# Routed attention with an ELU layer: the second mask of the first half of q moves from GpSimd to ScalarE

## The chip, the core and the metric

The kernel runs on one core of a Trainium2 chip. A core has five engines that run their own queues in order: TensorE (PE in the profile; PEld is its load of weights), VectorE (DVE), ScalarE (ACT), GpSimd (POOL) and SyncE (SP), which here only issues DMAs. The metric is device time in microseconds, the median of several runs. The profile is of one further execution.

## What is computed

Attention in which a query sees only the keys of its own cluster, followed by two matrix products with an ELU between them:

```python
q_assign = np.argmax(np.einsum('bhsd,hcd->bhsc', q_n, c_n), axis=-1)
k_assign = np.argmax(np.einsum('bhsd,hcd->bhsc', k_n, c_n), axis=-1)
mask = q_assign[:, :, :, None] == k_assign[:, :, None, :]
scores = scale * np.matmul(q, k.transpose(0, 1, 3, 2))
scores = np.where(mask, scores, -1000000000.0)
scores = scores - np.max(scores, axis=-1, keepdims=True)
attn = np.exp(scores)
attn = attn / (np.sum(attn, axis=-1, keepdims=True) + 1e-09)
return np.matmul(attn, v).astype(np.float32)
...
h = x @ w_in
g = np.where(h > 0.0, h, alpha * (np.exp(np.minimum(h, 0.0)) - 1.0))
return (g @ w_out).astype(np.float32)
```

There are 4 batches, 8 heads, 768 positions, a head size of 64 and 16 clusters per head. The layer has 3072 tokens, 512 channels and 2048 hidden ones. All is float32.

## The kernel before, in words

The attention runs over 32 blocks: 4 batches, two halves of q (384 rows each), four pairs of heads. For a block and each of 6 tiles of 128 keys, TensorE makes two plain score products (L510, one per head of the pair) and adds two masked products (L523) into the same bank; ScalarE takes the exponential (L532); in the next block TensorE multiplies the results with v (L548). VectorE adds the exponentials up (L535, L540, L541). Three pairs of banks go round in a ring (`pair_tiles`).

The mask is a product too. `assign` (L446) makes a one-hot code of the clusters of each row: VectorE turns the similarities (L453), takes the maximum over 16 clusters (L455), compares each value with it (L456, which also counts the hits) and turns the 0/1 codes back (L466). L456 reads two tiles that lie in SBUF, `sim` and `top`; the others read one. Two copies on ScalarE (L469) then put each half of the partitions into the other half, as side 1 of `hot_k` or `hot_q`. `mask_q` (L474) makes from `hot_q` two tiles `q_mask[half][:, :, x]`, x = 0 and 1, each a multiplication and an addition with a scalar per partition (`big`, `minus`): 0 where the cluster is the row's own, a huge negative number elsewhere. Tile x serves the pairs of heads with pr % 2 = x, so x = 0 serves the first block and x = 1 the second. In `mask_q` the masks of the first half of q in the first batch (b = 0, half = 0) are made by GpSimd (L478), all later ones by ScalarE (L480).

The order of the work is written out by hand: each engine executes its instructions in the order in which the code names them. Work that is to go to ScalarE or GpSimd a little later is put into the list `later` and issued by `flush()`. The start is `slot_first` (L632). There q and k of the first batch are turned by TensorE (`turned`, L622: products with the identity, then a copy by ScalarE at L630), and in this order:

- q is turned, and its clusters are found (`clusters_q(0, 0, d_bank)()`); the copies of L469 and both masks are put into `later`.
- The first 512 columns of k are turned for all four pairs of heads, and the remaining 256 for the first pair.
- The similarities of k's first 512 columns are computed into `o_bank`.
- `flush()` at L647 issues the copies for q on ScalarE and both masks on GpSimd.
- The remaining 256 columns of k are turned for the other three pairs (L648, L649), with three copies on ScalarE.
- The plain products of the first key tile (L651) and the similarities of k's last 256 columns into `d_bank` (L652) follow on TensorE.
- `told[0]()` (L653) is `assign` for k's first 512 columns on VectorE; the flush after it issues the copies of L469 for them on ScalarE.
- `told[1]()` is the same for the last 256. After three loads of SyncE's queue have been named, the loop over the six key tiles begins (L660).

The first masked product (L523) of the first block needs `hot_k` from L466, the second one side 1 of it from the first copy of L469.

After the attention the layer is computed in blocks with sums of sub-matrices, on all engines; nothing of that is edited.

Of the kernel before, what the change touches and what calls it, by code (L numbers as in the profile page):

```python
# [61 lines left out]
def main_path(ctx, tc, c, q, k, v, centroids, moe_w_in, moe_w_out, out):  # L62
# [118 lines left out]
    def load_k(b, pr):  # L181
        in_blocks(raw_k[pr % 2], k[b, 2 * pr : 2 * pr + 2])

    def load_q(b, half):
        for pr in range(NPR):
            in_blocks(raw_q[pr], q[b, 2 * pr : 2 * pr + 2, ts(half, HS)])
# [102 lines left out]
    def ask():  # L289
        nonlocal asked  # L290
        while asked < len(pieces):
            to, src = pieces[asked]
            if not wide:
                if asked == into and split < into:
                    return
                nc.sync.dma_start(to, src)
                asked += 1
                continue
            places[:] = [x for x in places if asked < x[1]]
            if not places:  # L300
                return
            place, limit = places.pop(0)
            w = place.rearrange("p a n -> p (a n)") if place.shape[1] == 1 else place
            n = to.shape[1]
            if place.shape[1] == 1:
                w = w.rearrange("p (f n) -> p f n", f=n)
            elif n == 1:
                src = src.rearrange("p a (f n) -> p (a f) n", f=place.shape[1])
            w = w.bitcast(U32)
            nc.sync.dma_start(w, src.bitcast(U32))  # L310
            words[asked] = (w.rearrange("p f (n w) -> p f n w", w=2), place, limit)
            asked_in[asked] = now
            asked += 1
# [56 lines left out]
    half = FC // 2  # L370
# [33 lines left out]
    credit, later, powers = 0.0, [], []  # L404

    def flush(*of):
        for others in of or (later, powers):
            for other in others:
                other()
            others.clear()  # L410
# [25 lines left out]
    def similar(t, cols, ps):  # L436
        for pr in range(NPR):
            nc.tensor.matmul(  # L438
                ps[32 * pr : 32 * pr + 32, : cols.stop - cols.start],
                lhsT=cT[:, 32 * pr : 32 * pr + 32],  # L440
                rhs=t[pr][:, cols],
                start=True,
                stop=True,
            )

    def assign(hot, ps):  # L446


        nonlocal counted
        size = hot.shape[2]  # L450
        n = size // NC
        sim, oh, top = told_in[size]
        nc.vector.transpose(sim, ps[:, :size])  # L453
        s = sim.rearrange("p (n c) -> p n c", c=NC)
        nc.vector.tensor_reduce(top, s, axis=Axis.X, op=Alu.max)  # L455
        nc.vector.scalar_tensor_tensor(  # L456
            oh.rearrange("p (n c) -> p n c", c=NC),
            s,
            1.0,
            top.unsqueeze(2).to_broadcast([P, n, NC]),  # L460
            op0=Alu.mult,
            op1=Alu.is_equal,
            accum_out=count[:, counted : counted + 1],
        )
        counted += 1
        nc.vector.transpose(hot[:, 0], oh)  # L466
        for e in range(2):
            later.append(
                lambda e=e: nc.scalar.copy(  # L469
                    hot[64 * (1 - e) : 64 * (1 - e) + 64, 1], hot[64 * e : 64 * e + 64, 0]  # L470
                )
            )

    def mask_q(b, half):  # L474
        for x in range(2):
            to, by, more = q_mask[half][:, :, x], big[:, x : x + 1], minus[:, x : x + 1]
            if (b, half) == (0, 0):
                nc.gpsimd.tensor_scalar(to, hot_q, by, more, op0=Alu.mult, op1=Alu.add)  # L478
            else:
                nc.scalar.activation(to, hot_q, Act.Identity, scale=by, bias=more)  # L480

    def clusters_k(b, half, ps):
        cols = slice(half * HS, half * HS + HS)
        if b == 0:
            cols = slice(half * CUT, S if half else CUT)
        similar(kT[b % 2], cols, ps)
        return lambda: assign(hot_k[b % 2][:, :, cols], ps)

    def clusters_q(b, half, ps):
        similar(qT[half], slice(0, HS), ps)  # L490

        def told():
            assign(hot_q, ps)
            later.append(lambda: mask_q(b, half))

        return told

# [3 lines left out]
    def ring():  # L501
        nonlocal turn_of
        turn_of = (turn_of + 1) % 3
        return pair_tiles[turn_of]

    def plain(n, kt, s):
        b, half, pr = blocks[n]
        for e in range(2):
            rows = slice(64 * e, 64 * e + 64)
            nc.tensor.matmul(  # L510
                s[:, e, :HS],
                lhsT=kT[b % 2][pr][rows, ts(kt, P)],
                rhs=qT[half][pr][rows],
                start=True,
                stop=False,
            )

    def masked(n, kt, s):
        b, half, pr = blocks[n]
        for e in range(2):  # L520
            rows = slice(64 * e, 64 * e + 64)
            side = int(pr // 2 != e)
            nc.tensor.matmul(  # L523
                s[:, e, :HS],
                lhsT=hot_k[b % 2][rows, side, ts(kt, P)],
                rhs=q_mask[half][rows, side, pr % 2],
                start=False,
                stop=True,
            )

    def exponential(kt, s):
        nc.scalar.activation(probs[kt], s[:, :, :HS], Act.Exp, scale=SCALE)  # L532

    def sums_begin():
        nc.vector.tensor_tensor(  # L535
            add_to, probs_all[:, : 4 * HS], probs_all[:, 4 * HS : 8 * HS], op=Alu.add
        )
# [76 lines left out]
    def turned_by_pe(to, t, n):  # L614
        for h in range(2):
            nc.tensor.matmul(  # L616
                to[D * h : D * h + D], lhsT=t[:, h, n], rhs=ident, start=True, stop=True
            )
# [3 lines left out]
    def turned(to, t, n):  # L622

        nonlocal turns
        bank = pair_tiles[turns % 3][:, turns // 3 % 2]
        turns += 1
        size = to.shape[1]
        for i in range(size // P):
            turned_by_pe(bank[:, ts(i, P)], t, n + i)
        nc.scalar.copy(to, bank[:, :size])  # L630

    def slot_first():  # L632

        for _ in range(6):
            nc.tensor.matmul(
                o_bank, lhsT=blank, rhs=blank[:, 0:1].to_broadcast([P, 512]), start=True, stop=True
            )
        for pr in range(NPR):
            turned(qT[0][pr], first_q[pr], 0)
        nc.tensor.transpose(o_bank[:, :P], work[:, : 2 * D], ident)  # L640
        nc.vector.tensor_copy(cT, o_bank[:, :P])
        clusters_q(0, 0, d_bank)()
        for pr in range(NPR):
            turned(kT[0][pr][:, :CUT], first_k[pr], 0)
        turned(kT[0][0][:, CUT:], first_k[0], CUT // P)
        told = [clusters_k(0, 0, o_bank)]
        flush()  # L647
        for pr in range(1, NPR):  # L648
            turned(kT[0][pr][:, CUT:], first_k[pr], CUT // P)  # L649
        first = ring()  # L650
        plain(0, 0, first)  # L651
        told.append(clusters_k(0, 1, d_bank))  # L652
        told[0]()  # L653
        flush()
        told[1]()
        load_k(1, 0)
        ask()
        load_q(0, 1)
        load_k(1, 1)
        for kt in range(NT):  # L660
            s = ring() if kt else first
            if kt:
                plain(0, kt, s)
            masked(0, kt, s)
            exponential(kt, s)
            if kt == 2:
                flush()
            elif kt == 3:
                sums_begin()
# [432 lines left out]
    class OutUnit:  # L1102
        of, width = "out", P
# [53 lines left out]
    class InUnit:  # L1157
        of, width = "in", 512
# [343 lines left out]
    def verdict():  # L1502
# [4 lines left out]
        nc.vector.tensor_copy(c["go"], ps[:1, :1])  # L1507

    slot_first()
    for n in range(1, len(blocks)):  # L1510
        slot(n)
# [334 lines left out]
```

## Time and profile before

| | us |
|---|---|
| median of 3 runs (lowest, highest) | 890.75 (890.51, 891.31) |
| the profiled execution, its own time | 889.33 |
| its span, first to last instruction | 887.5 |
| busy in the span: PE, DVE, ACT, POOL | 876.4, 711.5, 446.0, 228.3 |

The profile is read through views. The page gives each engine's busy share in 40 slices of the span and the chain of work that ended last, followed back from the last instruction to what released it. The chain can also be listed in order of time. The timeline lists the instructions of an engine with their start, their length, how many were merged (x3), and in brackets the idle time before them and what ended it. The view of one line gives the durations of its instructions, each form with its shape. "L456" is line 456 of the kernel; names such as `p_out<-o_bank` are what is written and what is read. Some tiles share memory under another name: `hot_q`, `hot_k` and the raw k and q of the start lie in `w_out`, the masks in `kq_g`.

### The profile page before, as it was taken

To read this page: it belongs to the slowest core of one execution; us is meant where nothing else is said; L and a number is where in the kernel's file an instruction comes from. 1 tells how busy PE (TensorE), PEld (TensorE's weight loads), DVE (VectorE), ACT (ScalarE), POOL (GpSimd) and SP (SyncE) were. 2 spreads that over 40 slices of the span, in tenths; PEclk is the share of its full clock that TensorE was granted. 3 is DMA by queue.
4 is the path that set the end of the run, shared out by engine and by line. 5 is a ranking of instruction groups with operands and counts; after the bars stand their busy time and mean duration, and the time that the engine had idled before them with its cause. 6 is when DMAs were issued, how large, how long until landed. Compare 5 with 4: busy or idle time off the path is not lost.

```text
span 887.5 us, 17035 instructions
## 1 busy us (share of the span) xinstructions
PE 876.4 (99%) x6437; PEld 677.6 (76%) x6441; DVE 711.5 (80%) x1041; ACT 446.0 (50%) x852; POOL 228.3 (26%) x294
## 2 busy tenths in 40 slices
PE   8999999999999999999999999999999999999996
PEld 5444444444444458899989999999999999999996
DVE  4789998999998997898688957884788478856784
ACT  6678786787768654412233235423542364236421
POOL 1011121121113566841332013601351135103200
PEclk9999999999999999999999999999999999999999
DMA  7766685466337342165677875186518761866171
GB/s 239 169 129 184 148 180 135 122 125 146 80 120 213 126 143 64 49 163 135 217 247 247 274 217 167 57 278 212 176 52 273 216 186 48 267 214 192 42 244 68
DMA packets 157370, 145.68 MB, mean 164 GB/s; under 512 B 89824, under 2 KB 109280, under 8 KB 156256
## 3 DMA queue, kind: packets, MB, share of 16 engines
q1 hardware_dynamic: 151584, 132.45, 50.5%
q0 software_dynamic: 5408, 11.54, 5.7%
q8 instruction: 53, 0.87, 0.4%
q10 hardware_dynamic: 288, 0.52, 0.2%
q14 instruction: 37, 0.30, 0.1%
HBM read 114.59 MB, written 21.50 MB: 153 GB/s over the span
## 4 chain that ended last, share of the span: by engine, by line
PE 93%; POOL 3%; issue 2%; DVE 1%; DMA 0%; ACT 0%; SPq 0%; POOLq 0%; ACTq 0%
PE bank L1086 23%; PE banks L510 15%; PE o_bank L548 14%; PE bank L796 12%; PE bank L1176 9%; PE o_bank L1086 4%; PE banks L523 4%; PE o_bank L796 2%; PE d_bank L1086 2%; PE o_bank L1176 2%; PE d_bank L568 1%; PE d_bank L438 1%; POOL kq_g L810 1%; PE d_bank L1176 1%; PE banks L616 1%
## 5 line engine op out<-in xcount | busy, mean ns | idle before, releaser
L532 ACT ACTIVATE p_out<-banks 128x768 f32<-128x768 f32 x192 | 154.0, 811 | 25.4 <-PE banks L523 24.2
L548 PE MATMUL o_bank<-p_out,kq_g 128*64 128x384 f32 x768 | 130.9, 490 | 0.0
L548 PEld LDWEIGHTS o_bank<-p_out,kq_g 128*64 128x64 f32 x768 | 52.3, 137 | 74.7 <-issue 70.3
L810 POOL TENSOR_SCALAR kq_g<-kq_g 128x512 f32<-128x512 f32 x96 | 69.1, 728 | 109.7 <-ACT kq_g L809 108.3
L535 DVE TENSOR_TENSOR sums_w<-p_out 128x1536 f32<-128x1536 f32 x32 | 59.1, 1847 | 10.3 <-ACT p_out L532 10.3
L796 PE MATMUL bank<-xT,spare 128*128 128x256 f32 x256 | 59.2, 379 | 0.0
L809 ACT ACTIVATE kq_g<-bank 128x512 f32<-128x512 f32 x68 | 39.8, 602 | 38.5 <-PE bank L796 18.4
L540 DVE TENSOR_TENSOR sums_w<-sums_w,p_out 128x1536 f32<-128x1536 f32 x32 | 56.2, 1757 | 3.3 <-DVE sums_w L535 0.5
L609 POOL DMA_DIRECT2D sums_w<-xT x28 | 17.7, 649 | 153.2 <-DVE xT L585 92.0
L1086 PE MATMUL bank<-w_out,kq_g 128*128 128x128 f32 x448 | 56.0, 275 | 0.3 <-DVE kq_g L813 0.3
L1086 PEld LDWEIGHTS bank<-w_out,kq_g 128*128 128x128 f32 x448 | 53.4, 192 | 0.8 <-DVE kq_g L813 0.5
L796 PEld LDWEIGHTS bank<-xT,spare 128*128 128x128 f32 x256 | 48.3, 190 | 6.4
L796 PE MATMUL bank<-x_sum,w_in 128*128 128x256 f32 x224 | 52.9, 379 | 0.0
L813 DVE SCALAR_TENSOR_TENSOR kq_g<-kq_g,bank 128x512 f32<-128x512 f32 x68 | 45.0, 680 | 7.7 <-POOL kq_g L810 7.7
L1194 POOL TENSOR_TENSOR spare<-x_sum 128x128 f32<-128x128 f32 x16 | 7.3, 457 | 154.4 <-PE bank L1176 88.8
L796 PEld LDWEIGHTS bank<-x_sum,w_in 128*128 128x128 f32 x224 | 42.6, 190 | 5.8
L1390 DVE TENSOR_TENSOR kq_g<-kq_g 128x1024 f32<-128x1024 f32 x36 | 43.9, 1221 | 0.0
L562 ACT ACTIVATE xT<-o_bank 128x384 f32<-128x384 f32 x32 | 15.6, 489 | 53.0 <-PE o_bank L548 53.0
L604 POOL TENSOR_TENSOR xT<-xT,sums_w 128x384 f32<-128x384 f32 x32 | 41.1, 1304 | 1.6 <-DMA sums_w<-xT 1.6
L510 PE MATMUL banks<-x_sum,xT 64*128 64x384 f32 x192 | 39.8, 492 | 0.0
L510 PE MATMUL banks<-kq_g,xT 64*128 64x384 f32 x192 | 39.6, 491 | 0.0
L510 PE MATMUL banks<-kq_g 64*128 64x384 f32 x192 | 39.6, 491 | 0.0
(379 smaller groups left out, 2027.5 us busy)
## 6 DMA issues: line engine op xcount, KB each, us to landing
kq_g<-in_v_dram SPq DMA_DIRECT2D x32, 384.0 KB, 3.8
sums_w<-far_s_s SPq DMA_DIRECT2D x42, 256.0 KB, 3.7
spare<-w_far SPq DMA_DIRECT2D x32, 256.0 KB, 3.0
words_w<-far_s_s SPq DMA_DIRECT2D x26, 256.0 KB, 3.1
out_dram<-p_out SPq DMA_DIRECT2D x22, 256.0 KB, 3.2
w_out<-in_q_dram SPq DMA_DIRECT2D x112, 48.0 KB, 2.5
sums_w<-xT POOLq DMA_DIRECT2D x28, 192.0 KB, 3.3
sums_w<-far_s_q SPq DMA_DIRECT2D x21, 256.0 KB, 3.5
```

The lines of the kernel that those rows point to most:

```text
L510: nc.tensor.matmul(s[:, e, :HS], lhsT=kT[b % 2][pr][rows, ts(kt, P)], rhs=qT[half][pr][rows], start=True, stop=False,)
L532: nc.scalar.activation(probs[kt], s[:, :, :HS], Act.Exp, scale=SCALE)
L535: nc.vector.tensor_tensor(add_to, probs_all[:, : 4 * HS], probs_all[:, 4 * HS : 8 * HS], op=Alu.add)
L540: nc.vector.tensor_tensor(add_to, add_to, probs_all[:, 8 * HS :], op=Alu.add)
L548: nc.tensor.matmul(o_bank[64 * e : 64 * e + 64, :HS], lhsT=v_raw[n % 2][:, e, kt], rhs=probs[kt][:, e], start=(kt == 0), stop=(kt == NT - 1),)
L604: nc.gpsimd.tensor_tensor(x_of(n), x_of(n), r, op=Alu.mult)
L796: nc.tensor.matmul(bank[:, ts(f, QS)], lhsT=left[:, ch, ts(f, P)], rhs=right[:, ch], start=first and f == 0 and ch == 0, stop=ch == 1, ski ...
L810: nc.gpsimd.tensor_scalar(to, to, 1.0, 0.0, op0=Alu.min, op1=Alu.max)
L813: nc.vector.scalar_tensor_tensor(to, to, -1.0, as_part(bank, to), op0=Alu.add, op1=Alu.max)
L1086: nc.tensor.matmul(bank[:, :P], lhsT=left[:, f], rhs=right[:, f], start=first and f == 0, stop=last and f == 3, skip_group_check=True,)
L1176: nc.tensor.matmul(bank[:, ts(f, P)], lhsT=left[:, ts(f, P)], rhs=right, start=m in ("m1", "m5") and f == 0, stop=True, skip_group_check=True,
L1390: nc.vector.tensor_tensor(b[to][:, f], b[x][:, f], b[y][:, f], op=op)
```

## The change

`mask_q` gets a parameter that says which of its two tiles to make, and its choice of engine now also asks for x = 0. The function that follows the clusters of q puts only x = 0 into `later` for the first half of q in the first batch. The tile x = 1 of that half is made by a call in `slot_first`, behind the turning of k's remaining columns and ahead of the first block's plain products; by the new condition it goes to ScalarE. All other halves keep both tiles on ScalarE, as before.

```diff
-    def mask_q(b, half):
-        for x in range(2):
+    def mask_q(b, half, of=range(2)):
+        for x in of:
             to, by, more = q_mask[half][:, :, x], big[:, x : x + 1], minus[:, x : x + 1]
-            if (b, half) == (0, 0):
+            if (b, half, x) == (0, 0, 0):
                 nc.gpsimd.tensor_scalar(to, hot_q, by, more, op0=Alu.mult, op1=Alu.add)
             else:
                 nc.scalar.activation(to, hot_q, Act.Identity, scale=by, bias=more)
...
         def told():
             assign(hot_q, ps)
-            later.append(lambda: mask_q(b, half))
+            later.append(lambda: mask_q(b, half, range(1 if (b, half) == (0, 0) else 2)))
...
         for pr in range(1, NPR):
             turned(kT[0][pr][:, CUT:], first_k[pr], CUT // P)
+        mask_q(0, 0, range(1, 2))
         first = ring()
         plain(0, 0, first)
         told.append(clusters_k(0, 1, d_bank))
```

## The prediction

> **What bounds the kernel now.** I read the page first, for the bound of the whole, then the chain of waits over the first 23 us, where the edited code runs, and then the timeline of each engine there.
>
> ```profile
> PE   8999999999999999999999999999999999999996
> PE 93%; POOL 3%; issue 2%; DVE 1%; DMA 0%; ACT 0%; SPq 0%; POOLq 0%; ACTq 0%
> ```
>
> The first line is TensorE's busy share in 40 slices of 22.2 us, the second the share of each engine in the chain that ended last. TensorE sets the end nearly everywhere, so anything that lets it start its unbroken run earlier moves the whole program. Its first slice is only 8 tenths busy: that is the start, where the change lies. The chain of waits there (start, length, what; us):
>
> ```profile
> 12.89 1.31 PE o_bank L438 x8
> ...
> 14.22 0.73 DVE p_out L453
> ...
> 14.97 0.70 DVE p_out L455
> ...
> 15.70 1.34 DVE p_out L456 x2
> ...
> 17.06 0.72 DVE w_out L466
> ...
> 17.81 0.62 ACT w_out L469
> ...
> 18.48 0.33 PE banks L523
> ```
>
> From 14.2 to 18.5 us the end is set not by TensorE but by VectorE: it turns the similarities of the first 512 rows of k, takes their maximum (L455), compares (L456), turns the result back (L466), and ScalarE copies half of it across (L469) before TensorE may do the second masked product. After 18.48 the chain is TensorE row upon row. Neither mask of L478 stands in the chain. That alone would say that moving one of them is worth nothing, so I looked at what runs beside the chain (timeline by engine; start, length, then the operation; what ended an idle time stands in brackets):
>
> ```profile
> 14.53 1.96 POOL L478 TENSOR_SCALAR kq_g<-w_out,big,minus 128x768 bf16<-128x768 bf16 x2 [13.16 <-ACT w_out L469]
> 14.82 1.27 ACT L630 COPY xT<-banks 128x256 f32<-128x256 f32 x3 [0.40 <-PE banks L616]
> 17.81 1.26 ACT L469 COPY w_out<-w_out 64x512 bf16<-64x512 bf16 x2 [1.71 <-DVE w_out L466]
> 17.83 0.33 PE L523 MATMUL banks<-kq_g,w_out 64*128 64x384 bf16 x1 [0.77 <-DVE w_out L466]
> 18.48 0.33 PE L523 MATMUL banks<-kq_g,w_out 64*128 64x384 bf16 x1 [0.32 <-ACT w_out L469]
> ```
>
> GpSimd makes both masks without a pause, 14.53 to 16.49, so the second one runs from about 15.51. ScalarE has done its copies of k at 14.82 + 1.27 = 16.09 and then has nothing for 1.71 us. TensorE idles 0.77 and 0.32 us at the end of the same stretch. Last, line 456 by form (duration ns min/median/max):
>
> ```profile
> L456 DVE SCALAR_TENSOR_TENSOR w_out<-w_out x15: 426/558/559, 10.2 to 265.4; 128x384 bf16<-128x384 f32 x14, 128x256 bf16<-128x256 f32 x1
> L456 DVE SCALAR_TENSOR_TENSOR p_out<-p_out x1: 1324/1324/1324, 15.7 to 15.7; 128x512 bf16<-128x512 f32 x1
> ```
>
> This is the row that matters. 256 columns take 426 ns and 384 take 558, so 128 columns cost 132 ns and 512 should take 558 + 132 = 690 ns. The one that stands in the chain took 1324: 634 ns too many. It starts at 15.70, while GpSimd is in its second mask. Its neighbours do not suffer: the maximum L455 takes 420, 553 and 686 ns at 256, 384 and 512 columns, exactly in line, though GpSimd's first mask ran beside part of it.
>
> **What the Trainium skill says.** The page "SBUF — State Buffer", section "Who interferes with whom", states that a VectorE instruction with two inputs in SBUF contends with a GpSimd instruction that reads SBUF, that an instruction with one input outside the 2-port modes does not, and its section on the two separate sides says that the pair of ports is an exclusive lock: whoever comes first has it for its whole instruction and "the other fully blocks". L456 has two inputs in SBUF (sim, and top spread out), L455 has one. The trace agrees to the hundredth: if L456 can do nothing until GpSimd ends at 16.49, what is left to its end at 17.02 is 0.53 us, a 690 ns instruction less its start-up. The same page says that ScalarE never waits on the shared ports, so the mask made there should not block VectorE in its turn; the many ScalarE rows beside VectorE rows here show no stretching. "Perfetto Trace Analysis", section "GPSIMD Engine Instruction", warns that a single span on GpSimd is unreliable and start-to-start spacing is better; here two back to back last 1.96 us, so 0.98 each is safe.
>
> **The change part by part.**
>
> 1. GpSimd loses its second mask (984 ns median of the two). Its next work is the DMA issue of L609 at 50.92, more than 34 us later, so its own time is worth nothing. What goes is the block on L456: 1324 - 690 = 0.63 us out of the chain. The first mask, 14.53 to 15.51, stays and ends 0.19 us before L456 starts, so it does not take the second one's place as blocker. Bounds for this term: 0 if L456 is slow for another reason, 0.65 if the instruction is a little shorter than the line through the two smaller sizes. I take 0.63.
>
> 2. ScalarE gains one ACTIVATE, 128x768 bf16. The same operation stands on L480 with 14 calls, median 1.02 us; two back to back occupy 1.95 us, so a follower can start about 0.93 us after it. It is put behind the last copy of k, so it can start at 16.09 to 16.12 and ends at about 17.12. Its inputs (both sides of hot_q) were written by 11.4 us (VectorE) and 14.42 us (ScalarE), big and minus at about 2.4 us. Behind it on ScalarE is L469, which is in the chain. Without the block, L466 starts at 15.70 + 0.69 + 0.04 = 16.43, takes 0.71, ends at 17.14, and L469 can start at 17.18 instead of 17.81. The mask is out of the way at 17.05 to 17.14. So it hides in what remains of ScalarE's idle time, with 0.04 to 0.13 us to spare. If it were longer by more than that, the excess would come off the gain one to one. Range of this part: 0 to -0.1 us; I take 0. No table load: L480 is the same function between exponentials, and the whole trace holds just the two loads of L248 and L249, both before 4.8 us.
>
> 3. The other waits at the join. The products of k's second part into d_bank run on TensorE until 16.43 + 0.64 = 17.07, so the first masked product, which waited for L466 until 17.83, can start at about 17.20; 0.13 of its 0.77 us of waiting are left. The second one follows L469's first copy, 17.18 + 0.62 + 0.05 = 17.85 instead of 18.48: again 0.63. VectorE goes on to the second part of k at about 17.07, right as d_bank is complete; its result is asked for by the fifth key tile, four exponentials later, and moves with the rest. The new mask itself is read first by the block of the second pair of heads, at 27.60 before, 10 us after it is made. DMAs: none is issued by the moved step, and SyncE's queue is not touched.
>
> 4. What is late next. After 18.48 the chain up to 337 us has TensorE rows almost alone, so the 0.63 us travel on, unless something stands at a fixed time. The candidate is SyncE's queue, which paces the 16 small loads of q from 17.54 to 33.5 by itself and issues the v of the third block only at 36.41. It lands within 4.3 us, by 40.7; the products that read it start at 41.74. The slack of 1.0 us shrinks to 0.4 and holds. The next, issued at 52.32, lands 5.5 us later at 57.8 for use at 61.44. Later loads of v wait for TensorE (17.7 us in that queue's waits up to 120 us), so they follow it.
>
> Sum: -0.63 us. The profiled execution took 889.33 us in all with a span of 887.5; it would become 888.7 with 886.9. The median of the runs shown is 890.75, 1.42 above the profiled one; the same step from it gives 890.12, so 890.1 us.
>
> **The rivals.**
>
> A, my case: the block on L456 goes and ScalarE hides the mask. 890.1 us.
>
> B: nothing arrives at the end. Either L456 is slow from its size or place in p_out (it is the only one of that form, which speaks for it; that L453, L455 and L466 at 512 columns lie on or below the line through their smaller sizes speaks against), or ScalarE's mask holds L469 back, or the v load at 40.7 us takes the gain. 890.75 us.
>
> C, slower: the start moves, and with it the order in which VectorE and GpSimd meet at their shared ports in the stage from 338 to 382 us, where the chain lies on GpSimd. There an L354 of VectorE starts at 339.01 and GpSimd's L775 at 339.02; the former took 2.49 us against 1.21 in its undisturbed group, so GpSimd had the ports. If GpSimd loses such a meeting it waits some 1.2 us, and the chain with it. This decides from two lost meetings on: 890.1 + 2.4 = 892.5. For it: starts 10 ns apart. Against: a uniform shift by 0.63 us changes no order, and the runs shown lie within 0.8 us.
>
> D, faster than A by such a meeting won: 890.1 - 1.2 = 888.9. For it: the L604 pairs in the attention take 1.96 or 2.33 us by chance of the meeting; against it, the same as for C.
>
> **How the numbers follow.** A has 0.70, B 0.11, C 0.09, D 0.10. A measurement of this kernel can tell about 0.2% from no change, here 1.8 us: below 889.0 is faster, above 892.5 slower. A and B lie inside, with a little of each side lost to the scatter of runs (0.8 us from lowest to highest). Faster is D, 0.11 with that scatter; slower is C, 0.09; the same 0.80. The range holds A and B with the scatter on both sides, 888.8 to 891.5; C is left out, and D lies at its lower edge.
>
> **What would show it.** Right: L456 of p_out near 690 ns; L478 once; a new row for ScalarE from about 16.1 to 17.1; L469 at about 17.18; the second masked product at about 17.85; all of the attention stage earlier by 0.6 us. Step 1 is wrong if L456 still takes 1.3 us with GpSimd idle. Step 2 is wrong if L469 starts later than 0.04 us after L466. Step 4 is wrong if the products of the third block wait for v, or if the shift seen at 300 us is not the one seen at 20 us. C or D show as a shift that changes between 338 and 382 us.

## The result: 0.23% faster, and not where the prediction put it

The changed kernel takes 888.75 us (median of 10 runs, 888.1 to 889.62) against 890.9 us for the kernel before, measured beside it (median of 10 runs, 890.51 to 891.98). The ratio is 0.9977 with a 95% interval of 0.9969 to 0.9985: 2.15 us faster, where 0.63 us were forecast; the time lies at the lower edge of the forecast range (888.8 to 891.5), 0.05 us under it. The profiled execution of the changed kernel took 889.50 us with a span of 887.7, so its span is not shorter than that of before (887.5). The two profiles, each a single execution, hide the gain; they have to be taken apart.

The start first. The chain of waits of the changed kernel, 12 to 24 us (start, length, what; us):

```profile
13.95 1.31 PE o_bank L438 x8
...
15.28 0.73 DVE p_out L453
...
16.03 0.70 DVE p_out L455
...
16.75 0.71 DVE p_out L456 x2
...
17.49 0.72 DVE w_out L466
...
18.23 0.62 ACT w_out L469
...
18.90 0.33 PE banks L523
```

From L453 to the second masked product it is 3.62 us (15.28 to 18.90), before it was 4.26 (14.22 to 18.48): 0.64 us less, all of it in L456, 1.34 to 0.71. But everything here stands 1.06 us later than in the profile of before, because the loads of q landed later in this execution (in the profile of before TensorE waited for them too). What ScalarE and GpSimd do beside it, by the timeline of each engine:

```profile
15.58 0.98 POOL L478 TENSOR_SCALAR kq_g<-w_out,big,minus 128x768 bf16<-128x768 bf16 x1 [14.21 <-ACT w_out L469]
15.88 1.27 ACT L630 COPY xT<-banks 128x256 f32<-128x256 f32 x3 [0.40 <-PE banks L616]
17.17 1.03 ACT L480 ACTIVATE kq_g<-w_out,minus,big 128x768 bf16<-128x768 bf16 x1
18.23 1.26 ACT L469 COPY w_out<-w_out 64x512 bf16<-64x512 bf16 x2
```

The mask on ScalarE ends at 18.20, just as L466 does (17.49 + 0.72), and L469 starts 0.02 us after that. The cover that was forecast holds, with nothing to spare. Line 456 of the changed kernel by form:

```profile
L456 DVE SCALAR_TENSOR_TENSOR p_out<-p_out x1: 692/692/692, 16.8 to 16.8; 128x512 bf16<-128x512 f32 x1
```

So the start does what was forecast: 692 ns, estimated 690. Next, between 40 and 45 us, a wait that before does not have (us in total, times, longest):

```profile
PE o_bank L548 <- DMA kq_g<-in_v_dram: 0.7, 1, 0.7
```

The products of the third block waited for their v, and this execution lost there what it had won. Matched instruction by instruction, TensorE then stays 1.18 us behind the execution of before to the end. Yet the span is only 0.3 us longer. The other 0.9 us are found after the last product, in the stretch that is called the tail below. The chain of waits ends, before and then in the changed kernel, with the last addition:

```profile
880.17 0.29 DVE p_out L1397
```

```profile
881.36 0.29 DVE p_out L1398
```

From there to the end of the span it is 7.0 us before (887.5 - 880.46) and 6.1 us after (887.7 - 881.65). The last instructions of ScalarE and SyncE, by line, show why; before first, then the changed kernel (count, ns min/median/max, first to last start in us):

```profile
L57 ACTq EVENT_SEMAPHORE  x1: 17/17/17, 884.1 to 884.1; - x1
...
L1842 SPq DRAIN  x3: 7/7/12, 884.6 to 886.9; - x3
...
L1842 ACTq DRAIN  x2: 8/72/135, 886.5 to 886.9; - x2
```

```profile
L57 ACTq EVENT_SEMAPHORE  x1: 17/17/17, 885.5 to 885.5; - x1
...
L1843 SPq DRAIN  x3: 7/7/13, 886.9 to 887.2; - x3
...
L1843 ACTq DRAIN  x2: 8/8/8, 885.6 to 887.2; - x2
```

L57 is the branch over the general path at the program's end; the DRAIN after it is where the engines meet before the program closes (they meet twice, so each has a later DRAIN too). Before, ScalarE had passed its semaphore instruction at 884.1 and came to its DRAIN only at 886.5, some 2.4 us later, with nothing to do in between; the others, SyncE the last of them, had been ready since 884.7. In the changed kernel 0.1 us lie between the two, and SyncE, which waits for the output to land, is the last, at 886.9. ScalarE's queue has one instruction more than before (1184 against 1183); the instructions at its end are the same.

### The profile page after: what moved, and what is told of

Same layout as the page of the kernel before. It is cut to its first block, busy times and chain, and to the rows that moved or that the text cites. A ratio compares the mean times of both kernels' runs of the same rounds, so it can differ in the third digit from the quotient of the medians.

```text
span 887.7 us, 17035 instructions
## 1 busy us (share of the span) xinstructions
PE 876.6 (99%) x6437; PEld 677.6 (76%) x6441; DVE 710.7 (80%) x1041; ACT 447.0 (50%) x853; POOL 227.3 (26%) x293
## 4 chain that ended last, share of the span: by engine, by line
PE 92%; POOL 3%; issue 2%; DVE 1%; DMA 1%; ACT 0%; SPq 0%; POOLq 0%; ACTq 0%
PE bank L1087 23%; PE o_bank L548 15%; PE banks L510 14%; PE bank L797 12%; PE bank L1177 9%; PE o_bank L1087 4%; PE banks L523 3%; PE o_bank L797 2%; PE d_bank L1087 2%; PE o_bank L1177 2%; PE d_bank L568 1%; PE d_bank L438 1%; POOL kq_g L811 1%; PE d_bank L1177 1%; PE banks L616 1%
## 5 line engine op out<-in xcount | busy, mean ns | idle before, releaser
L810 ACT ACTIVATE kq_g<-bank 128x512 f32<-128x512 f32 x68 | 39.8, 602 | 38.5 <-PE bank L797 18.4
L510 PE MATMUL banks<-x_sum,kq_g 64*128 64x384 f32 x192 | 39.6, 491 | 0.0
```

The source lines that it names most:

```text
L510: nc.tensor.matmul(s[:, e, :HS], lhsT=kT[b % 2][pr][rows, ts(kt, P)], rhs=qT[half][pr][rows], start=True, stop=False,)
```

## The experiments

Two theories. **T**: the gain has two parts, L456 and the tail; the tail depends on how many instructions ScalarE's queue holds, not on which. **R**: all comes from the start. A third part, **V**, was added later: v of the third block takes back a part of what L456 gains. Each kernel was measured beside the kernel before.

**One instruction more, nothing else** (kernel before):

```diff
+    pad = const.tile([P, 1], F32, name="pad")
...
         slot(n)
+        if n == 1:
+            nc.scalar.copy(pad, ones[:, :1])
```

> The kernel before with one tiny copy (128x1) added to ScalarE's queue, in its idle time of the second block; both masks stay with GpSimd. Theory T (the change gains twice: 0.63 us from the block on L456, and some 1.5 to 2 us at the program's end, because one more ScalarE instruction shifts its code against the pieces in which it is fetched): L456 at 512 columns still 1.3 us, but ScalarE's DRAIN comes within 0.2 us of its semaphore instruction of L57 instead of 2.5 us after it; the time falls by 1.0 to 2.0 us. Rival R (the whole gain comes from the start, the place of the code means nothing): no change, within 0.4 us of before.

Measured: 888.89 us against 890.65, ratio 0.9981 (0.9973 to 0.9989). A copy of one column that nobody reads makes the kernel 1.76 us faster. The comparison of L456 (L457 in this kernel) still takes 1324 ns; ScalarE's end:

```profile
L57 ACTq EVENT_SEMAPHORE  x1: 17/17/17, 884.5 to 884.5; - x1
...
L1845 ACTq DRAIN  x2: 8/8/8, 884.6 to 886.1; - x2
```

R falls here.

**The block on L456 alone** (kernel before; in GpSimd's queue a copy of the count of k's second part stands ahead of the second mask, so that it starts only when both L456 are done):

```diff
-            later.append(lambda: mask_q(b, half))
+            later.append(lambda: mask_q(b, half, range(1 if (b, half) == (0, 0) else 2)))
...
         told[1]()
+        nc.gpsimd.tensor_copy(mark, count[:, 2:3])
+        mask_q(0, 0, range(1, 2))
```

> The kernel before with the second mask still on GpSimd, but behind the count of the second half of k, so that it cannot meet L456; ScalarE's queue has as many instructions as before. Theory T: L456 takes 0.69 us, the tail still has ScalarE's 2.5 us before its DRAIN; the time falls by 0.6 us (0.2 to 1.0). Rival R: the whole gain of the change, 2.1 us, is here.

Measured: 890.66 against 890.65, ratio 1.0002 (0.9994 to 1.001). L456 took 694 ns, as forecast:

```profile
L456 DVE SCALAR_TENSOR_TENSOR p_out<-p_out x1: 694/694/694, 16.6 to 16.6; 128x512 bf16<-128x512 f32 x1
```

So neither its size nor its place in `p_out` made it slow. But nothing arrived at the end. The waits of 40 to 45 us held what the changed kernel's had, though less of it:

```profile
PE o_bank L548 <- DMA kq_g<-in_v_dram: 0.2, 1, 0.2
```

**Both together**, with no mask on ScalarE:

> Both edits together: GpSimd's second mask late, and the tiny copy on ScalarE; ScalarE makes no mask. Theory T: the whole gain of the change, 2.1 us (1.5 to 2.7), as the sum of the two edits alone. Rival R: as the late mask alone. A third theory, that ScalarE's making of the mask matters by itself: less than the change's gain.

Measured: 888.55 against 890.65, ratio 0.9975 (0.9966 to 0.9984): the whole gain, without ScalarE making any mask of this half. So ScalarE's making of the mask isn't needed for the gain: a queue that is one instruction longer, and GpSimd out of L456's way, are enough.

**The block made longer**, GpSimd's second mask made once more behind the first two:

```diff
-        for x in range(2):
+        for x in (0, 1, 1) if (b, half) == (0, 0) else (0, 1):
```

> The kernel before with GpSimd's second mask made twice over, same result. Both masks run one after the other, 15.5 to 17.5 us, so that L456 is blocked for a further 0.98 us. Theory of the exclusive ports with a plain chain behind: L456 at 512 columns takes 2.3 us, and the time rises by 0.98 us (0.5 to 1.4). If L456 is slow for its size or place: unchanged, 0. If a delay at the start grows on the way: more than 1.5 us.

Measured: 890.76 against 890.65, ratio 1.0001 (0.9993 to 1.001). My first theory's number was wrong, and the timeline tells why:

```profile
15.96 3.35 POOL L478 TENSOR_SCALAR kq_g<-w_out,big,minus 128x768 bf16<-128x768 bf16 x3 [14.59 <-ACT w_out L469]
```

```profile
17.13 1.32 DVE L456 SCALAR_TENSOR_TENSOR p_out<-p_out 128x512 bf16<-128x512 f32 x1
```

Three masks of 0.98 us take 3.35 instead of 2.94 us, and L456 takes 1.32 as before: the second mask ends at 17.92 and L456 0.53 us later, just as in the kernel before, and GpSimd's third takes 1.30 us. This fits a lock that is handed over between instructions: L456 loses what is left of one mask, though another is queued behind it, and the third mask waits for L456. The run therefore doesn't tell how a longer delay travels. Its time alone would also fit "slow for its size or place"; the late mask rules that out.

**v of the third block asked for earlier.** SyncE issues it behind four loads of k that nobody needs for long; these are put behind it:

```diff
         load_q(0, 1)
-        load_k(1, 1)
...
             load_v(n + 1)
+        if n == 1:
+            load_k(1, 1)
```

In the kernel before:

> The kernel before with one edit on SyncE's queue: the four loads of k for the second pair of the second batch come behind the load of v for the third block, so that this v is asked for some 2.7 us earlier. Theory V (what L456 gains is partly lost where the third block's products wait for v): in the kernel before this v is early enough in nearly all executions, so no change, within 0.3 us. Rival W (v is late in the kernel before as well): 0.3 to 1 us faster.

Measured: 890.46 against 890.68, ratio 0.9998 (0.999 to 1.0007): no change. Together with the late mask:

> GpSimd's second mask late, and v of the third block asked for earlier. Theory V: the 0.63 us that L456 gains reach the end, so 0.63 us below the kernel before (0.3 to 0.9), no wait for v at the third block. Rival X (the gain of L456 is lost somewhere else, or was none): no change, within 0.2 us.

Measured: 890.17 against 890.68, ratio 0.9995 (0.9987 to 1.0003). In the changed kernel:

> The changed kernel with the same edit on SyncE's queue. Theory V: some 0.3 us faster than the changed kernel, that is 2.4 us (2.0 to 2.8) below the kernel before, and no wait for v at the third block. Rival X: as the changed kernel, 2.1 us below before.

Measured: 888.04 against 890.68, ratio 0.9972 (0.9961 to 0.9983), the lowest ratio of all, though not apart from the changed kernel's by more than the intervals. Each single step here is smaller than its interval. What the profiles show is sharper. In every profile TensorE needs 23.27 us (23.26 to 23.27) from the second masked product of the first block to the products of the third, unless it waits for v; from there to the last product it is the same to 0.02 us in all but one profile (two copies, 0.27 us more). The table gives, for all kernels in which L456 is free, when v was asked for, when it landed, when the products began, and how much of that was waiting (us):

| kernel | v asked for | v landed | products begin | wait |
|---|---|---|---|---|
| changed kernel | 38.14 | 42.88 | 42.92 | 0.76 |
| changed kernel, again | 37.38 | 41.17 | 41.64 | 0 |
| late mask | 37.76 | 42.29 | 42.34 | 0.30 |
| late mask, again | 38.18 | 42.38 | 42.42 | 0.37 |
| late mask and copy | 37.63 | 41.39 | 41.84 | 0 |
| changed kernel, one fewer (below) | 38.50 | 42.76 | 42.80 | 0.33 |
| late mask, v earlier | 35.12 | 39.08 | 42.17 | 0 |
| changed kernel, v earlier | 34.65 | 38.47 | 41.91 | 0 |

In the six without the edit the wait is 0 to 0.76 us, 0.29 in the mean. Of the 0.63 us some 0.34 are left on average, and with v earlier all of them. In the kernels where L456 is blocked v was never late: it landed 0.76 us or more ahead of its use.

**One instruction fewer on ScalarE.** If the place decides, it can be moved the other way:

```diff
-            if (b, half) == (0, 0):
+            if (b, half) == (0, 0) or (b, half, x) == (0, 1, 1):
                 nc.gpsimd.tensor_scalar(to, hot_q, by, more, op0=Alu.mult, op1=Alu.add)
```

> The kernel before with one ScalarE instruction fewer instead of one more: the second mask of the second half of q in the first batch is made by GpSimd, at about 53 us, where it has nothing else; L456 is blocked as before. Theory T (the place of ScalarE's last instructions in the fetched pieces decides on the tail): the pair of semaphore instruction and DRAIN is no longer parted, the tail is short, 1.5 us (1.0 to 2.0) below before. Rival (the tail needs a later place, not just another): no change, DRAIN 2.5 us late as before.

Measured: 890.11 against 890.68, ratio 0.9993 (0.9985 to 1.0001). By its time a miss: 0.6 us faster, within the interval of no change, where 1.5 us were forecast. By its end half a miss, and the most telling run for the mechanism. ScalarE's end by line:

```profile
L57 ACTq EVENT_SEMAPHORE  x1: 17/17/17, 885.4 to 885.4; - x1
...
L1842 ACTq DRAIN  x2: 8/32/56, 885.5 to 888.3; - x2
L1842 ACTq EVENT_SEMAPHORE  x2: 17/17/17, 888.2 to 888.5; - x2
```

The DRAIN comes at once, as forecast, but now the instruction after it, the semaphore of the meeting, is the one that is 2.7 us late (885.5 to 888.2). The gap has moved by exactly one instruction. In both kernels the late one is the 1180th instruction that ScalarE executes: the DRAIN of 1183, the next semaphore of 1182. In the changed kernel the 1180th is the semaphore of L57, straight behind the branch, where ScalarE spends 2.8 us in any case (2.6 to 2.9 in all profiles) and SyncE still waits for the output to land.

**Two copies instead of one**:

> The kernel before with two tiny copies on ScalarE, one in the second and one in the third block. Theory T: two more instructions shift the end as one does, the parting of ScalarE's last instructions lies further ahead, inside the time in which SyncE waits for the output to land: 1.8 us (1.4 to 2.2) below before, ScalarE's semaphore of L57, DRAIN and next semaphore without a gap of 2 us between them. Rival (the copy of the second block did something by its place): another gain than with one copy, by more than 0.5 us.

Measured: 888.82 against 890.58, ratio 0.9981 (0.9974 to 0.9988), as with one. The 1180th instruction is now the branch itself, and no gap follows but the one behind the branch.

**Repetitions** of the changed kernel and of the late mask:

> The changed kernel once more, for its time beside the others of this call and a second profile. Theory V: as first measured, 2.15 us (1.6 to 2.7) below before, that is 0.1 to 0.5 us better than the two copies; v of the third block lands within 1 us of the time at which the products ask for it, ahead or behind. Rival X (nothing of L456's gain arrives): as the two copies.

Measured: 888.12 against 890.58, ratio 0.9973 (0.9963 to 0.9983). It is 0.7 us better than the two copies, a little more than forecast, with intervals that overlap.

> The kernel before with GpSimd's second mask late once more, since it had gained 0.0 where 0.6 was forecast. Theory V: a gain between 0 and 0.4 us, less than with v asked for earlier (0.5), and v of the third block about as late as the products ask for it. Rival X: the earlier result was scatter, 0.6 us.

Measured: 889.98 against 890.58, ratio 0.9993 (0.9985 to 1.0002). By its median this run speaks for rival X, but its profile shows the wait for v (0.37 us in the table). The two runs of the late mask gave 0.0 and 0.6 us; the intervals of both hold 0.34 us, and they hold 0 as well, so the times of these runs alone do not show it.

**The changed kernel with ScalarE's queue as long as before**, the test of it all: the same edit as for one instruction fewer, made in the changed kernel.

> The changed kernel with ScalarE's queue brought back to the number of instructions that it had before the change: the second mask of the second half of q in the first batch goes from ScalarE to GpSimd, which is idle there. L456 stays free and ScalarE still makes the mask that the change gave it. Theory T: ScalarE's DRAIN is again some 2.5 us behind its semaphore instruction of L57, from the last product to the end of the span it takes 7.2 to 7.9 us instead of 6.2, and only 0.35 us (0 to 0.7) of the gain is left against the kernel before. Rival R (the gain of the change comes from its start or from ScalarE's mask): 2 us below before.

Measured: 890.5 against 890.64, ratio 0.9995 (0.9987 to 1.0004). The change without its additional instruction gains 0.14 us, as theory T forecast, and the gain of 2.15 us is gone. Its end by line:

```profile
L57 ACTq EVENT_SEMAPHORE  x1: 17/17/17, 885.3 to 885.3; - x1
...
L1843 ACTq DRAIN  x2: 8/72/136, 888.4 to 888.8; - x2
```

There are 3.1 us between the two, and the tail is 8.16 us, a little above its forecast. Over all profiles, the time from the end of the last product to the end of the span:

| ScalarE's instructions | profiles | us from the last product to the end |
|---|---|---|
| 1182 | 1 | 7.21 |
| 1183 | 7 | 7.34 to 8.16, mean 7.70 |
| 1184 | 5 | 5.96 to 6.42, mean 6.20 |
| 1185 | 1 | 6.19 |

With 1183 to 1185 instructions the span ends 0.81 or 0.95 us after the first meeting's later DRAIN, ScalarE's or SyncE's. With 1183 it is ScalarE's, 1.6 to 2.1 us behind SyncE's; with more it is SyncE's. Not all of those 1.6 to 2.1 us are won, because with 1184 SyncE's own DRAIN came later too, 5.39 us after the last product in the mean against 4.91: the output landed later. Why it did is not shown.

The sum for the change: 7.70 - 6.20 = 1.50 us in the tail and 0.34 from the start, 1.84 us; measured were 2.15 (1.3 to 2.8) and 2.46 (1.5 to 3.3). The missing 0.3 and 0.6 us lie inside the intervals; the start of an execution moves by up to 1.4 us with the landing of q from profile to profile, so 14 profiles cannot weigh them, and no run settles what they are.

What parts the two instructions is not named by the profile. That ScalarE's code is brought in by pieces, and that the piece with the DRAIN is asked for only when ScalarE gets close to it, fits all of it: the fixed place, the 2.5 to 3.1 us without a cause, and the similar time that ScalarE needs after its branch before its next instruction (881.4 to 884.1 us before). The queue of instruction packets can be read in the same way. In the last stretch, before from 884 (with what was moved in slices of 0.1 us) and the changed kernel from 885 us, it shows:

```profile
GB/s 0 0 0 0 0 82 82 0 0 0 0 0 0 0 0 0 0 0 0 0 0 0 0 0 0 0 0 0 0 0 0 82 0 0 0 0 0 0 0 0
...
q14 instruction: 3, 0.02, 1.9%
```

```profile
q14 instruction: 2, 0.02, 1.7%
```

In all profiles two packets begin 0.6 to 0.9 us after the first instructions of VectorE and ScalarE behind the branch; before, these are at 884.0 and 884.1 and the packets at 884.6 and 884.7. The third appears in all eight profiles with 1182 or 1183 ScalarE instructions and in none with more. It begins 0.65 to 0.92 us after the late instruction (before at 887.2, the DRAIN being at 886.5), so it is not what ScalarE waited for: it would be the next piece, asked for when ScalarE has come into a new one, and the piece with the DRAIN would be one of the two before. The size of the pieces can be estimated as 128 instructions: in every profile one of this queue's packets of 8 KB begins within 2.6 us of each 128th ScalarE instruction, counted from the 63rd or 64th up to the 1088th. A packet does not tell for which engine it is, so the mechanism is argued from this, while the effect of the count is shown.

## Why the prediction was right and wrong

**What bounds the start, and step 1** were right: the block on L456 was read off a duration that was out of line with its other sizes, 1324 against 690 ns, and 692 is what came. The start-up that the prediction takes off (0.53 for 0.69 us) is the part that doesn't depend on the columns: 426 ns at 256 columns less twice 132 are 162 ns. The first mask did not take the second one's place. The late mask shows that the block goes with GpSimd's timing alone.

**Step 2** was right: one ACTIVATE of 1.03 us ending with L466, 0.62 us for L469's first copy behind it, no table load (L630, L480 and L469 follow one another). The margin forecast as 0.04 to 0.13 us was 0.03, just under it (18.20 to 18.23).

**Step 3** was right: from the start of L453 to the two masked products 2.98 and 3.63 us were forecast (14.22 to 17.20 and 17.85), and 2.97 and 3.62 were measured; the local gain is 0.64 us.

**Step 4** failed in its size. It said that the slack of v, 1.0 us, "shrinks to 0.4 and holds". Both numbers came from one profile of before, in which v had been asked for at 36.41 us; in the other profiles with SyncE's queue unchanged it was 36.7 to 38.5. The view gave landing times for two loads together; the first of them alone landed at 40.27, so the slack in that execution was even 1.5 us, and it still did not hold elsewhere. The third block waited for v in four of six profiles of kernels with L456 free and SyncE's queue unchanged, which takes the 0.63 us down to some 0.34 in the mean. The prediction had this as part of its rival B.

**The sum** failed by a term that it did not have. The greater part of the gain, 1.5 us by the profiles and 1.76 by the tiny copy, lies after the last product, where the prediction never looked: it said of the end only that TensorE sets it. The line of TensorE's busy share that it quotes could have led there: it remarks on the 8 of the first slice and not on the 6 of the last. The last product ended at 880.14 and the span at 887.5, 7.3 us in which TensorE does nothing, and the gap before ScalarE's DRAIN was there in the profile of before. What could not have been read from it is that one more instruction would close the gap.

**The rivals.** C and D put a change into the order of the meetings between 338 and 382 us. It did not happen: both traces keep their offset of 1.18 us through that stage and to the last product. L354 and GpSimd's L775 (L776 in the changed kernel) meet in the same order again, and L354 takes 2.49 us again. So "faster", which had only D and the scatter behind it, came true for a reason that no rival named, and that the measured time stands so close to the forecast range is luck: the edge it stands at was put there for D and the scatter.

## What to carry to other kernels

When an instruction beside a moved one takes longer than its size explains, look for what shared its ports; the gain is real locally, but ask in more than one execution whether a load with a fixed time takes it back. Read the stretch after the last product as its own stage: here the engines waited 1.8 us for the DRAIN of one that had nothing to do. And before a gain or loss of 0.1 to 0.3% is put down to what an edit does, add an idle instruction to the same queue: if that gives it too, it comes from the length of the queue and not from the work that was moved.

## What the runs showed of the hardware that had not been expected

- The number of instructions in ScalarE's queue moves the end of this program by 1.5 us: 1183 instructions end in 7.34 to 8.16 us after the last product, 1184 and 1185 in 5.96 to 6.42. With 1182 the gap stands one instruction later. The change without its additional instruction gained 0.14 us, within the interval.
- In the one run that tests it, VectorE and GpSimd handed the shared ports over between instructions. With three GpSimd operations of 0.98 us back to back, L456 waited for the rest of one (1324 ns in all, just as with two), and GpSimd's third then took 1.30 us, as if it waited for L456. The Trainium skill, "SBUF — State Buffer", section "Summary: rules for kernel authors", says that when a VectorE instruction has two inputs in SBUF and the GpSimd one reads SBUF, the second to issue blocks until the first finishes; that agrees, and this run adds that a further instruction queued on GpSimd did not keep the ports.
- The same load of v, behind the same queue, was asked for between 36.4 and 38.5 us and landed between 40.3 and 42.9 in eleven profiles. The slack of 1.0 us that was read from one profile was less than this spread of 2.6 us.
